# Tile 0 normalised in two halves, and three of its products in front of tile 1's turns

## The chip, the cores and the metric

The kernel runs on one core of a Trainium2 chip. The metric is the device time of one execution in microseconds (us); lower is better. The core has five engines that run on their own and wait for each other through semaphores: TensorE (PE, matmuls and transposes), VectorE (DVE), ScalarE (ACT), GpSimd (POOL) and SyncE (SP), which here issues most DMAs. Each engine works through its own queue in the order in which the program gives it work; an instruction that waits holds up everything behind it in that queue.

## The reference

The input x is 2048 tokens by 512 features. It is normalised over its features, and two blocks read the result: linear attention with 32 heads of 16, and a two-layer perceptron with a squared ReLU of width 1376. Both are added to x.

```python
xn = _layernorm(x)                                 # (x - mean) / sqrt(var + 1e-5)
q, k, v = split(xn @ wqkv)                         # 32 heads of 16
phi = lambda t: where(t > 0, t + 1, exp(t)) + 1e-6
kv  = einsum("bhsd,bhse->bhde", phi(k), v)
num = einsum("bhqd,bhde->bhqe", phi(q), kv)
den = einsum("bhqd,bhd->bhq", phi(q), phi(k).sum(s)) + 1e-6
A   = (num / den) @ wo
h   = xn @ w1 + b1
B   = square(max(h, 0)) @ w2 + b2
out = x + A + B
```

## The kernel before

All matmuls on the long path take their operands as a high and a low part (`fp32r` tiles, the low one the rest of the value), and a product is the sum of three passes: high by high, low by high, high by low. `split`, `heads_k`, `rests_k` and `transposed` make such parts: ACT or DVE copies the high one, DVE or POOL subtracts it for the low one.

The 2048 tokens are 16 tiles of 128 (`NT`), in blocks of four. The program has three stages: a start that brings in the first tiles, a loop over the tiles 2 to 15 (line 787) that projects k and sums k times tokens into four banks (`kx`), and two rounds of q, perceptron and output over two blocks each. The order on every engine is written out by hand: there is no planner, and an instruction stands in its engine's queue where the program calls it.

The change lies in the start. What happens there, with the lines:

- Eleven matmuls on zeros (L515), seen in the trace as 22, keep PE at work while the first loads are under way. The loads go through SP: tiles 0 and 1, the k columns of `wqkv` in four chunks (`rk`), tiles 2 and 3.
- `measure` (L230, L231) takes a tile's mean and variance on DVE. `roots` (L241, L242) makes one over the root of variance plus 1e-5 on POOL, as a power of -0.5.
- `normalise` (L264) subtracts the mean and multiplies by the root on DVE, one instruction for a tile of 128 by 512.
- `turned_pe` (L304) turns a tile with four transposes on PE. For tiles 0 and 1 they go into two banks of two chunks each, so that what follows can start on half a tile. It also sets the tile's last column to one (`ones`, L342, on POOL), behind the transposes.
- `transposed` gives three functions for a tile: `high(k)` copies half k of the turned tile on ACT (L320), `low(k)` subtracts that copy from it on DVE (L323), `keep_t` copies the whole for a store to memory (L330).
- `heads_k(j)` makes the high part of chunk j of the k weights (L562; chunk 0 on DVE, the others on ACT), `rests_k` its low part (L566; chunk 0 on POOL, the others on DVE).
- `some(i, u, js)` multiplies part u (0 high, 1 low) of tile i by the high part of the weight chunks in `js`, `rest(j, ...)` the high part of the tile by the low part of chunk j. Each is one matmul of 128 by 512 for a chunk, all into the bank `pk` of the tile.
- A copy of one element on POOL (L591) writes tile 1's result into the buffer of the tiles 4 to 7, so that the load of these tiles, which follows on SP, waits for it.
- Behind this stand the products of tile 2, `phi_k` (exponential and ReLU of k), `tokens` and `parts` (high and low parts of the normalised tile and of phi(k)), and `kx(0)`, the first sum (L385).

Of the kernel before, what the change touches and what calls it, by code (L numbers as in the profile page):

```python
# [10 lines left out]
OP = mybir.AluOpType  # L11
# [7 lines left out]
def kernel(  # L19
# [30 lines left out]
    nc = tc.nc  # L50
    xf = x.rearrange("b s d -> (b s) d")
    of = out.rearrange("b s d -> (b s) d")
    S, D = xf.shape
# [49 lines left out]
    def gjc(ap):  # L103

        return ap.rearrange("p (j g c) -> p g j c", j=NJ, g=NJ)
# [3 lines left out]
    def copy(eng, o, i, bias=0.0):  # L109
        if eng == "act":  # L110
            nc.scalar.activation(o, i, AF.Copy, bias=bias)  # L111
        elif bias:
            ENG[eng].tensor_scalar(o, i, bias, None, op0=OP.add)
        else:
            ENG[eng].tensor_copy(o, i)
# [41 lines left out]
    def load_x(i, t):  # L157
        n = t.shape[1]
        nc.sync.dma_start(t, xf[i * P:(i + n) * P, :].rearrange("(i p) d -> p i d", i=n))
        for k in range(n):  # L160
            xr[i + k] = t[:, k]
# [82 lines left out]
    def normalise(tiles, st, mv, y):  # L244

        n = len(tiles)
        r, u = (y[:, k, :n] for k in range(2))
        if tiles[-1] >= NPE:

            nc.vector.scalar_tensor_tensor(u, mv[:, :n, 0], -1.0, r, op0=OP.mult, op1=OP.mult)  # L250
        later = []

        def last(i, o, src, k):
            nc.scalar.activation(o, src, AF.Identity, bias=u[:, k:k + 1], scale=r[:, k:k + 1])
            if i in groups:
                regroup(i)

        for k, i in enumerate(tiles):
            o, src = xp[i], xr[i]
            if i >= NDVE:  # L260

                o, src = o.rearrange("p g (j c) -> p g j c", j=NJ), gjc(src)
            if i < NPE:
                nc.vector.tensor_scalar(o, src, mv[:, k, 0:1], r[:, k:k + 1], op0=OP.subtract, op1=OP.mult)  # L264
                if i in groups:
                    regroup(i)
            else:
                later.append(lambda a=(i, o, src, k): last(*a))
        return later
# [3 lines left out]
    def regroup(i):  # L273

        src, G = groups[i]
        via = dram.tile([P, NJ, src.shape[-1]], F32, name=f"via{i}")
        nc.sync.dma_start(via, src)
        of_g = via.rearrange("(r t) g n -> g t r n", r=NJ)
        for g in range(NJ):
            moves.append((G[32 * g:32 * (g + 1)], of_g[g]))  # L280
# [27 lines left out]
    def transposed(i, n=1):  # L308

        b, at = i // TB, slot(i)  # L310
        if i < NDVE:
            t = turned_pe(i, n)
        else:
            t = [xT[b][:, :, at] if i >= NPE else w512(f"t{i}", "p", 6).rearrange("p (j t) -> p j t", j=NJ)]
            turn(t[0], xg[i])
        m = NJ // n
        h, l = ([x[:, k * m:(k + 1) * m, at] for k in range(n)] for x in cols(i))

        def high(k=0):
            nc.scalar.activation(h[k], t[k], AF.Copy)  # L320

        def low(k=0):
            nc.vector.tensor_tensor(out=l[k], in0=t[k], in1=f32(h[k]), op=OP.subtract)  # L323

        def keep_t():
            o = t[0]
            if i < NDVE:
                o = w512(f"t{i}", "p", 6).rearrange("p (j t) -> p j t", j=NJ)
                for k in range(n):
                    copy("act", o[:, k * m:(k + 1) * m], t[k])  # L330
            if i < NPE:
                nc.sync.dma_start(xTd[b][:, :, at], o)

        return high, low, keep_t
# [27 lines left out]
    def project(i, ps, w, steps, first=True, last=True):  # L362

        for n, (j, u, v) in enumerate(steps):
            nc.tensor.matmul(ps, lhsT=cols(i)[u][:, j, slot(i)], rhs=w[v][:, j, :], start=first and n == 0,  # L365
                             stop=last and n == len(steps) - 1)
# [172 lines left out]
    for i0 in range(0, NT, TB):  # L539
# [6 lines left out]
        if i0 < NPE:  # L546
            i = i0 + TB - n - 1
# [3 lines left out]
        o = work.tile([P, n, 512], F32, name=f"xg{i0}", tag="r0" if i0 + TB == NT else "r3" if i0 >= NPE else "rc")  # L551
        for k in range(0, n, 2):
            i = i0 + TB - n + k
# [6 lines left out]
    def heads_k(*js, eng="act"):  # L560
        for j in js:
            copy(eng, wk[0][:, j, :], rk[:, j])  # L562

    def rests_k(eng, *js):
        for j in js:
            ENG[eng].tensor_tensor(out=wk[1][:, j, :], in0=rk[:, j], in1=f32(wk[0][:, j, :]), op=OP.subtract)  # L566
# [3 lines left out]
    def some(i, u, js, first=False):  # L570
        project(i, pks[i], wk, [(j, u, 0) for j in js], first, False)
# [6 lines left out]
    for t in two_tiles:  # L578
        measure(t)
        roots(*t)  # L580
    normalise(*two_tiles[0])
    high, low, keep0 = transposed(0, 2)
    high()
    heads_k(0, eng="dve")
    rests_k("pool", 0)
    some(0, 0, (0,), True)
    normalise(*two_tiles[1])
    high1, low1, keep1 = transposed(1, 2)
    heads_k(1)

    nc.gpsimd.tensor_copy(x4[:, 0, :1], xp[1][:, :1])  # L591
    load_x(4, x4)
    some(0, 0, (1,))
    low()
    some(0, 1, (0, 1))
    high(1)
    high1()
    low(1)
# [15 lines left out]
    some(1, 0, (2,))  # L614
    rest(1)
    normalise(*third)
    rests_k("dve", 2)
    some(1, 1, (2,))
# [8 lines left out]
    high, low, keep2 = transposed(2)  # L627
# [159 lines left out]
    for i in range(2, NT):  # L787
# [15 lines left out]
        if i < NDVE:  # L803
            high, low, keep_t = transposed(i + 1)
# [104 lines left out]
    for n in range(2):  # L909
# [124 lines left out]
        for p in range(NO + 1):  # L1034
            at_p = AT[p]
            kind, k = order[p] if p < NO else ("", 0)
            fa, fb = 2 * k, 2 * k + 1

            was, k = order[p - 1] if p else ("", 0)
# [209 lines left out]
        for e, f in enumerate(waiting[:-2]):  # L1249
# [14 lines left out]
            if n == 0 and 1 <= e < 5:  # L1264
                k, u = divmod(e - 1, 2)
# [68 lines left out]
```

## Time and profile before

| | before |
|---|---|
| median of 3 runs | 413.56 us (413.45 to 413.88) |
| profiled execution | 413.58 us |
| its span, first to last instruction | 411.9 us |
| granted TensorE clock | 1.00 |
| PE busy | 407.2 us (99%) |
| PE weight loads busy | 336.8 us (82%) |
| DVE busy | 311.1 us (76%) |
| ACT busy | 265.2 us (64%) |
| POOL busy | 59.0 us (14%) |
| data moved by DMA | 55.15 MB, mean 134 GB/s |

The profile is that of one execution. Its page gives the busy time of each engine, the chain of work that ended last, and groups of instructions. The views used here are the list of waits (which engine sat idle until which other was done), the table by stage (busy time of each engine between two times), the groups by line and shape, and the timeline: one row for each instruction or for several alike in a row, with start, duration, engine, line, operation, what is written and what is read, shape, count, and in brackets idle time of the engine before it with what ended it. Times in the timeline count from the start of the span. A line is often that of a helper, so the tile's name tells more than the line does.

### The profile page before, as it was taken

The page shows a single profiled execution, that of the slowest core. Times are in us where ns is not written, and L with a number is a line of the kernel's source. Part 1 is how long each engine was busy: PE and PEld are TensorE (multiplying, and loading weights), DVE is VectorE, ACT ScalarE, POOL GpSimd, SP SyncE. Part 2 cuts the span into 40 slices and gives each one's busy share as a digit, 9 for nine tenths or more (in the row PEclk, how much of TensorE's full clock was granted, in tenths as well). Part 3 has the DMA queues.
Part 4 walks back from the last instruction along what each step waited for, and adds up shares of the span by engine and source line. Part 5 has one row for each costly group of instructions (what it writes and reads, how often), then busy time and mean ns, then how long its engine had stood idle before and what let it go on. Part 6 is the DMA issues. An engine that isn't in the chain of part 4 may idle for free.

```text
span 411.9 us, 5395 instructions
## 1 busy us (share of the span) xinstructions
PE 407.2 (99%) x1831; PEld 336.8 (82%) x1831; DVE 311.1 (76%) x555; ACT 265.2 (64%) x465; POOL 59.0 (14%) x91
## 2 busy tenths in 40 slices
PE   8999999999999999999999999999999999999996
PEld 7788888888888888888878888888888888878885
DVE  5885567797899898988449995567989686449843
ACT  4757677656678779788637631577588857737520
POOL 5542233230410000030000140100000200000210
PEclk9999999999999999999999999999999999999999
DMA  6979672810412221273366992411121880024602
GB/s 221 344 230 338 171 306 103 254 28 2 124 60 71 79 73 56 77 198 58 134 237 241 382 183 87 118 53 51 51 78 28 231 197 32 2 98 157 103 1 102
DMA packets 45661, 55.15 MB, mean 134 GB/s; under 512 B 8001, under 2 KB 29761, under 8 KB 44354
## 3 DMA queue, kind: packets, MB, share of 16 engines
q1 hardware_dynamic: 43330, 50.61, 37.3%
q0 software_dynamic: 2304, 4.20, 6.4%
q8 instruction: 14, 0.23, 0.2%
q14 instruction: 13, 0.11, 0.1%
HBM read 41.43 MB, written 13.37 MB: 133 GB/s over the span
## 4 chain that ended last, share of the span: by engine, by line
PE 98%; DMA 1%; DVE 0%; POOL 0%; issue 0%; ACT 0%
PE acc L130 37%; PE b L484 32%; PE pk L365 11%; PE kx L385 11%; PE acc L495 2%; PE pz L130 1%; PE pkv L885 1%; PE pm L130 1%; PE pz0b L130 1%; PE b L130 1%; DMA x<-in_A_x_dram 1%; PE pt L304 1%; PE acc L502 0%; PE end L130 0%; DVE st L230 0%; POOL y L242 0%
## 5 line engine op out<-in xcount | busy, mean ns | idle before, releaser
L130 PE MATMUL acc<-w2r,s 128*128 128x512 f32 x477 | 112.8, 390 | 0.0
L130 PEld LDWEIGHTS acc<-w2r,s 128*128 128x128 f32 x477 | 89.4, 188 | 19.3 <-issue 0.7
L484 PE MATMUL b<-T,aop 128*128 128x512 f32 x336 | 83.4, 389 | 0.0
L484 PEld LDWEIGHTS b<-T,aop 128*128 128x128 f32 x336 | 63.1, 188 | 13.2
L385 PE MATMUL kx<-pk,tok 128*128 128x512 f32 x192 | 46.5, 391 | 0.0
L385 PEld LDWEIGHTS kx<-pk,tok 128*128 128x128 f32 x192 | 35.8, 188 | 7.7 <-ACT pk L111 0.3
L1015 POOL DMA_DIRECT2D res<-in_B_b_dram x16 | 14.3, 1123 | 181.5 <-DVE dt L426 64.2
L484 PE MATMUL b<-xs0h,aop 128*128 128x512 f32 x112 | 36.9, 390 | 0.0
L130 PE MATMUL acc<-mh,aTsr 128*128 128x512 f32 x112 | 35.6, 389 | 0.0
L1023 DVE TENSOR_TENSOR res<-acc,res 128x512 f32<-128x512 f32 x16 | 11.0, 692 | 23.0 <-PE acc L130 18.4
L119 POOL TENSOR_TENSOR tok<-xp,tok 128x512 fp32r<-128x512 f32 x16 | 21.2, 1327 | 43.2 <-ACT tok L111 43.2
L122 DVE TENSOR_TENSOR w2r<-r,w2r 128x512 fp32r<-128x512 f32 (+2 forms) x35 | 25.6, 734 | 0.1
L484 PEld LDWEIGHTS b<-xs0h,aop 128*128 128x128 f32 x112 | 21.0, 188 | 4.4
L130 PEld LDWEIGHTS acc<-mh,aTsr 128*128 128x128 f32 x112 | 21.0, 188 | 4.4
L111 ACT ACTIVATE aop<-S 128x512 fp32r<-128x512 f32 x28 | 17.5, 623 | 11.0 <-DVE S L714 11.0
L119 DVE TENSOR_TENSOR aop<-S,aop 128x512 fp32r<-128x512 f32 x28 | 19.5, 697 | 4.8 <-ACT aop L111 4.4
L119 DVE TENSOR_TENSOR s<-c,s 128x512 fp32r<-128x512 f32 x20 | 13.6, 689 | 11.5 <-ACT s L111 11.5
L130 PE MATMUL acc<-ml,aTsr 128*128 128x512 f32 x56 | 21.8, 389 | 0.0
L484 PE MATMUL b<-xs0l,aop 128*128 128x512 f32 x56 | 21.8, 389 | 0.0
L111 ACT ACTIVATE w2r<-r 128x512 fp32r<-128x512 f32 x32 | 19.6, 619 | 2.4 <-DMA out_dram<-res 2.0
L111 ACT ACTIVATE T<-Tf 128x512 fp32r<-128x512 f32 x16 | 9.5, 624 | 16.5 <-DVE Tf L657 16.4
L484 PE MATMUL b<-xs1h,aop 128*128 128x512 f32 x56 | 19.5, 389 | 0.0
(195 smaller groups left out, 769.3 us busy)
## 6 DMA issues: line engine op xcount, KB each, us to landing
r<-in_B_w_dram SPq DMA_DIRECT2D x49, 256.0 KB, 2.9
res<-in_A_x_dram SPq DMA_DIRECT2D x8, 512.0 KB, 4.6
res<-in_B_b_dram POOLq DMA_DIRECT2D x16, 256.0 KB, 5.5
out_dram<-res SPq DMA_DIRECT2D x15, 256.0 KB, 2.1
via<-xp SPq DMA_DIRECT2D x5, 512.0 KB, 3.0
xg<-via SPq DMA_DIRECT2D x20, 128.0 KB, 2.6
xTd<-t SPq DMA_DIRECT2D x8, 256.0 KB, 4.3
x<-in_A_x_dram SPq DMA_DIRECT2D x4, 512.0 KB, 6.9
```

Of the source, the lines that this page charges most:

```text
L111: nc.scalar.activation(o, i, AF.Copy, bias=bias)
L119: ENG[el].tensor_tensor(out=l, in0=src, in1=f32(h), op=OP.subtract)
L122: nc.vector.tensor_tensor(out=l, in0=src, in1=f32(h), op=OP.subtract)
L130: nc.tensor.matmul(ps, lhsT=a[u], rhs=b[v], start=first and n == 0, stop=last and n == 2)
L304: nc.tensor.transpose(t[k][:, at:at + P], xp[i][:, j * P:(j + 1) * P], ident)
L365: nc.tensor.matmul(ps, lhsT=cols(i)[u][:, j, slot(i)], rhs=w[v][:, j, :], start=first and n == 0, stop=last and n == len(steps) - 1)
L385: nc.tensor.matmul(kxp[c], lhsT=tok[i][:, u, c * P:(c + 1) * P], rhs=pk[i][:, v], start=i == 0 and (u, v) == first, stop=i == NT - 1 and ( ...
L484: nc.tensor.matmul(ps, lhsT=a[u][:, j * P:(j + 1) * P], rhs=b[v][:, j, :], start=first and j == 0 and n == 0, stop=last and j == 1 and n == 2,
L495: nc.tensor.matmul(ps, lhsT=s[u][:, k * P:(k + 1) * P], rhs=w2s[NF - 1][u][:, a:z], start=first and u == 0, stop=stop and u == 1)
L885: nc.tensor.matmul(ps[:, at], lhsT=wvs[:, c, at], rhs=kxs[c // 2][:, c % 2, at], start=c == 0 and j == 0, stop=c == NJ - 1 and j == NJ - 1 ...
L1015: nc.gpsimd.dma_start(r[:, i], b2[None, :].partition_broadcast(P), accum_op=OP.add)
L1023: nc.vector.tensor_tensor(out=r[:, a:z], in0=ps, in1=r[:, a:z], op=OP.add)
```

## The change

Two things are changed, both in the start. In `normalise`, tile 0 is done as two instructions of 256 columns each, where every other tile stays one instruction. In the written order, three products of tile 0 (low by weight chunk 0, high by weight chunk 1, after the high by chunk 0 that already stood there) come in front of tile 1's norm and turns, and with them `low()`, the subtraction for the first half of tile 0, which stands on DVE in front of tile 1's norm; `heads_k(1)` is called ahead of these products. The fourth product (low by chunk 1) stays behind tile 1's turns.

```diff
@@ normalise @@
             if i < NPE:
-                nc.vector.tensor_scalar(o, src, mv[:, k, 0:1], r[:, k:k + 1], op0=OP.subtract, op1=OP.mult)
+                for part in (slice(0, D // 2), slice(D // 2, D)) if i == 0 else (slice(None),):
+                    nc.vector.tensor_scalar(o[:, part], src[:, part], mv[:, k, 0:1], r[:, k:k + 1],
+                                            op0=OP.subtract, op1=OP.mult)
                 if i in groups:
                     regroup(i)
@@ the start @@
     heads_k(0, eng="dve")
     rests_k("pool", 0)
     some(0, 0, (0,), True)
+    low()
+    some(0, 1, (0,))
+    heads_k(1)
+    some(0, 0, (1,))
     normalise(*two_tiles[1])
     high1, low1, keep1 = transposed(1, 2)
-    heads_k(1)
 
     nc.gpsimd.tensor_copy(x4[:, 0, :1], xp[1][:, :1])
     load_x(4, x4)
-    some(0, 0, (1,))
-    low()
-    some(0, 1, (0, 1))
+    some(0, 1, (1,))
     high(1)
     high1()
     low(1)
```

## The prediction

> **What bounds the kernel now.** I read the page first, then the waits of the first 30 us, then a table by stage, then the timelines of the first 17 us, one engine at a time.
>
> ```profile
> span 411.9 us, 5395 instructions
> ...
> PE 98%; DMA 1%; DVE 0%; POOL 0%; issue 0%; ACT 0%
> ```
>
> The span is 411.9 us and the profiled run took 413.58 us, so 1.68 us lie outside the span; the median of the three runs, 413.56, is 0.02 us below the profiled run. TensorE (PE) carries 98% of the chain that ended last. The change touches only the first 9 us, so the question is whether PE waits anywhere near it, and whether it could make up a delay later.
>
> ```profile
> PEld pk L365 <- ACT xs1h L320: 0.7, 2, 0.5
> ...
> PEld kx L385 <- ACT pk L111: 0.3, 1, 0.3
> ...
> PE pk L365 <- ACT xs1h L320: 0.3, 1, 0.3
> PE pt L304 <- DVE xp L264: 0.2, 1, 0.2
> ```
>
> Apart from the start of the warm-up these are the only waits of PE and its weight loads (PEld) in that stretch, and all stand before the first kx matmul: the transposes of tile 0 wait for its norm, the first k product and later the first of tile 2 for ACT's copy, and kx(0) for ACT's part of pk.
>
> ```profile
> 16.19:22.23 6.04, 6.04 (x29) 5.00 (x29) 5.08 (x10) 4.91 (x10) 2.92 (x5) 1.00 0.90 307
> 350.00:400.00 50.00, 50.00 (x226) 40.90 (x225) 32.88 (x56) 27.76 (x47) 5.12 (x6) 1.00 0.28 74
> ```
>
> From 16.19 us on, PE is busy for all of a stage (6.04 of 6.04, 50.00 of 50.00), at a granted clock of 1.00. So there is nothing in which a later start could be absorbed: **what the first kx matmul gains or loses, the kernel gains or loses**. Now the timelines (start, duration, then engine, line, operation).
>
> ```profile
> 0.83 4.85 PE L515 MATMUL warm<-const-float32-0.0 128*128 128x128 f32 x22 [0.83 <-PEq L1320]
> 5.88 0.66 PE L304 MATMUL pt<-ident,xp 128*128 128x128 f32 x4 [0.20 <-DVE xp L264]
> 6.79 0.50 PE L365 MATMUL pk<-wkh,xs1h 128*128 128x512 f32 x1 [0.26 <-ACT xs1h L320]
> 7.13 0.60 PE L304 MATMUL pt<-ident,xp 128*128 128x128 f32 x4
> 7.49 0.47 PE L365 MATMUL pk<-wkh,xs1h 128*128 128x512 f32 x1
> ...
> 8.49 0.40 PE L365 MATMUL pk<-wkh,xs1h 128*128 128x512 f32 x1
> ...
> 16.19 3.02 PE L385 MATMUL kx<-pk,tok 128*128 128x512 f32 x12
> ```
>
> ```profile
> 5.28 0.55 DVE L264 TENSOR_SCALAR xp<-x,mv,y 128x512 f32<-128x512 f32 x1 [0.23 <-POOL y L242]
> 5.74 0.42 DVE L115 CAST wkh<-rk 128x512 fp32r<-128x512 f32 x1
> 6.30 0.55 DVE L264 TENSOR_SCALAR xp<-x,mv,y 128x512 f32<-128x512 f32 x1
> 6.77 0.42 DVE L323 TENSOR_TENSOR xs1l<-pt,xs1h 128x256 fp32r<-128x256 f32 x1
> 7.56 0.83 DVE L323 TENSOR_TENSOR xs1l<-pt,xs1h 128x256 fp32r<-128x256 f32 x2 [0.37 <-ACT xs1h L320]
> 8.50 0.69 DVE L230 BATCH_NORM_STATS2 st<-x 128x6 f32<-128x512 f32 x1
> ...
> 10.75 0.55 DVE L264 TENSOR_SCALAR xp<-x,mv,y 128x512 f32<-128x512 f32 x1 [0.43 <-POOL y L242]
> 11.21 1.28 DVE L566 TENSOR_TENSOR wkl<-rk,wkh 128x512 fp32r<-128x512 f32 x2
> 12.42 0.69 DVE L230 BATCH_NORM_STATS2 st<-x 128x6 f32<-128x512 f32 x1
> ...
> 14.32 0.55 DVE L264 TENSOR_SCALAR xp<-x,mv,y 128x512 f32<-128x512 f32 x1 [0.42 <-POOL xp L342]
> 14.79 0.68 DVE L360 SCALAR_TENSOR_TENSOR k<-pk,k 128x512 f32<-128x512 f32 x1
> 15.39 0.68 DVE L230 BATCH_NORM_STATS2 st<-x 128x6 f32<-128x512 f32 x1
> ```
>
> ```profile
> 6.36 0.38 ACT L320 ACTIVATE xs1h<-pt 128x256 fp32r<-128x256 f32 x1 [4.29 <-PE pt L304]
> ...
> 15.50 0.63 ACT L111 ACTIVATE pk<-k 128x512 fp32r<-128x512 f32 x1 [0.45 <-DVE k L360]
> ```
>
> ```profile
> 5.53 0.73 POOL L242 TENSOR_TENSOR y<-y,power 128x1 f32<-128x1 f32 x1
> 6.60 0.28 POOL L342 MEMSET xp<- 128x1 f32 x1 [0.34 <-PE pt L304]
> 6.69 1.30 POOL L566 TENSOR_TENSOR wkl<-rk,wkh 128x512 fp32r<-128x512 f32 x1
> ...
> 10.15 0.57 POOL L242 TENSOR_TENSOR y<-y,power 128x1 f32<-128x1 f32 x1
> ...
> 13.72 0.57 POOL L242 TENSOR_TENSOR y<-y,power 128x1 f32<-128x1 f32 x1
> ```
>
> Read backwards from kx(0) at 16.19: it waits for ACT's high half of pk at 15.50, that for VectorE's (DVE's) phi at 14.79, which stands behind the norm of tile 3 at 14.32, which waits for POOL's power at 13.72 to 14.29; POOL waits for the statistics of tile 3 at 12.42; these stand behind the two rests of wk from 11.21 and the norm of tile 2 at 10.75, which waits for POOL's power at 10.15 to 10.72; and that for the statistics of tile 2 at 8.50. From 8.50 to 16.19 DVE and POOL pass work to each other without slack. PE's own work ends just ahead and then waits 0.3 us. So **the start of tile 2's statistics (8.50 us) decides**. In DVE's queue it stands behind the low halves of tile 0 and tile 1 (6.77 and 7.56), and the last of these needs tile 1's norm (6.30), its transposes (7.13) and ACT's copy.
>
> **The change, part by part.**
>
> *Two halves of tile 0's norm.* One instruction more on DVE. No row shows a 256-wide norm; the form's ends are 512 elements (0.55 at 5.28) and the nearest small one:
>
> ```profile
> L1106 DVE TENSOR_SCALAR zc<-zc 128x4 f32<-128x4 f32 x2 | 0.3, 156 | 0.0
> ```
>
> A line between 0.156 for 4 and 0.55 for 512 gives 0.35 for 256. It cannot be under 0.28, half of the whole; the 256-wide subtraction at 6.77, with a PSUM source, took 0.42, which is the other end. I take 0.35, since it is the same operation. Neighbours overlap by 0.09 (5.74 against 5.83), so the halves end at 5.63 and 5.89. The warm matmuls end at 5.68 (0.83 + 4.85); transposes came 0.05 behind the norm, so the first two start at 5.68 instead of 5.88, the last two at 5.94, and all four end near 6.32 instead of 6.54. ACT's copy moves from 6.36 to 6.16 and ends at 6.54; the first k product moves from 6.79 to 6.59. The cast of wk at 5.74 moves to 5.80 and ends at 6.22, still ahead of 6.59: nothing lost. So far a gain of 0.20 us on PE.
>
> *Tile 0's low half in front of tile 1's norm.* It needs ACT's copy, so it starts 0.03 behind it, at 6.57. Behind it in DVE's queue stand tile 1's norm, both other low halves, tile 2's statistics and so the whole chain above. The norm started at 6.30 and can now start only 0.41 behind the low half (the spacing of the pair at 7.56), at 6.98: 0.68 later, for a norm that depends on nothing in that low half.
>
> *What the norm meets there.* POOL's 1.30 us subtraction (L566, the rest of wk chunk 0) ran from 6.69 to 7.99, just after the norm. It stands behind the memset of tile 0's ones column, 0.06 behind the end of the transposes; with these at 6.32, the memset is at 6.38, the subtraction at 6.47 to 7.77. So the norm, which came in front of it, now comes in the middle of it. What that costs is shown by two other pairs of rows:
>
> ```profile
> 17.88 1.29 POOL L119 TENSOR_TENSOR tok<-xp,tok 128x512 fp32r<-128x512 f32 x1 [1.46 <-ACT tok L111]
> 18.74 0.98 DVE L373 SCALAR_TENSOR_TENSOR pk<-k,pk 128x512 fp32r<-128x512 f32 x1
> ```
>
> ```profile
> L373 DVE SCALAR_TENSOR_TENSOR pk<-k,pk 128x512 fp32r<-128x512 f32 x11 | 7.6, 690 | 3.1 <-ACT pk L111 2.7 <-PE kx L385 0.2
> ```
>
> The usual duration of that DVE form is 0.69; beside a POOL subtraction that ended at 19.17 it took 0.98 and ended at 19.72, 0.55 behind it. It had been held until POOL was through, with 0.14 of its 0.69 done before. The other way round:
>
> ```profile
> L342 POOL MEMSET xp<- 128x1 f32 x16 | 1.7, 109 | 0.3 <-PE pt L304 0.3
> ```
>
> A memset of one column takes 0.109 in the mean; the one at 6.60 took 0.28 and ended at 6.88, 0.04 behind tile 1's norm. So a norm on DVE and work on POOL exclude each other. No row shows a norm as the one held; a plain bound below is that it isn't held (0), above that it waits to POOL's end and then needs 0.41 (0.55 less 0.14). I take held, because the norm itself held POOL at 6.60. What is left after POOL's end lies between 0.28 (half of 0.55) and 0.41; I take 0.35. The norm ends at 7.77 + 0.35 = 8.12 instead of 6.85, 1.27 late.
>
> The Trainium skill's page "SBUF — State Buffer", section "Who interferes with whom", speaks against this change at just this place: VectorE and GpSimd share one pair of ports, a tensor_scalar between SBUF tiles can run in a mode that takes it, and whichever issued first keeps it for its whole instruction. By that rule the sum is the one made here; the rows above agree with it for the subtraction held by POOL and for the memset held by the norm.
>
> *Three products in front of tile 1's turns.* The same number of matmuls; PE meets the second product at 6.59 + 0.34 = 6.93 (the first spacing, 6.79 to 7.13) and waits for the low half until 6.57 + 0.42 + 0.05 = 7.04, with two products and the turns queued behind it. The third product needs ACT's wk chunk 1, which follows the first copy on ACT as before. Both are through by about 7.6, and PE then waits for tile 1's norm until 8.17. That waiting is no cost by itself; it matters through what follows.
>
> *The sum.* ACT's copy of tile 0 came 0.48 behind the first transpose (5.88 to 6.36) and takes 0.38: tile 1's at 8.65 to 9.03. Its low half starts at 9.06, and tile 2's statistics 0.40 behind that, at 9.46 instead of 8.50: **0.96 late**. Every link from there to kx(0) keeps its length, so kx(0) starts at 17.15. PE's own delay is less (the first product of tile 1 at 9.08 instead of 8.49, 0.59 late) and hides in that wait. With 0.96 on the profiled run: 413.58 + 0.96 = 414.54, and 414.5 as a median. With the ends of the two unknown durations (halves 0.28 and 0.42, the rest of the held norm 0.28 and 0.41) it is 0.85 to 1.2, that is 414.4 to 414.8.
>
> *What moves along at no price.* POOL's ones column of tile 1 and the one-element copy that releases the load of tiles 4 to 7 wait for tile 1's turns, so SyncE issues that load about 1 us later, with the stores of the turned tiles and the later x loads behind it in SP's queue.
>
> ```profile
> x<-in_A_x_dram SPq DMA_DIRECT2D x1, 1024.0 KB, 5.2
> ```
>
> Its issue was at 8.18, and 5.2 makes it land at 13.4; its first reader is at 15.39. With both 1 us later the cover of 2 us stays; without it, each us late would go to kx(0). ACT's wk chunks 2 and 3 come behind tile 1's copies and about 1 us late, with PE late as well.
>
> There is one more thing that could collide: POOL's power for tile 1 (5.53) took 0.73 beside the norm and the cast. If it slips in between the two halves, the second half waits up to 0.3 us, everything behind it too: 414.8 to 414.9.
>
> **The rivals.**
>
> First, **the norm isn't held** by POOL. For it: no row shows a norm held. Against it: the memset at 6.60. Then the norm runs from 6.98 to 7.53, the turns at 7.58, ACT's copy at 8.06 to 8.44, the low half at 8.47, the statistics at 8.87: 0.37 late, 413.9. This is slower still, but by less than can be told.
>
> Second, the other side, **no slower: PE decides the start**. The place is the stretch between tile 2's statistics and kx(0). The three products let PE work while tile 1 is late, and its first product is 0.20 us earlier; if the chain DVE-POOL had 0.96 us to spare there, kx(0) would come 0.20 earlier, 413.4. It decides from the point at which that spare exceeds the delay of the statistics. For it: PE's only wait in the stretch before kx(0) is 0.3 us and some of 0.2. Against it: the norms at 10.75 and 14.32 each follow POOL's power by 0.03 us, which is no spare at all.
>
> Third, **the clock falls back**. The 22 warm matmuls (128 columns) took 4.85 us, 0.22 each, the four transposes from 7.13 to 7.49, 0.09 each, so the clock opened in between, after about 4.5 us of work. PE now has a gap of some 0.6 us before tile 1's turns. If it closed there and needed 4.5 us again, half of that is lost: 2.3 us more, 416.8. Against it: gaps of 0.2 and 0.3 us at this place left the granted clock at 1.00. The Trainium skill's page "TensorE: Matmul & The Clock Gate", section "HAM oscillation — how this bites in real kernels", names gaps beyond about 3.4 us as what closes it; by that rule nothing closes here.
>
> That the change isn't what it says cannot be: the built order of each engine has the two halves, the three products and the norm behind the low half, as written.
>
> **How the numbers follow.** The forecast (held) has a chance of 0.81, of which about 0.1 is for the collision of the power; the norm not held 0.14; PE decides 0.03; the clock 0.02. The difference that a measurement of this kernel can tell from none is about 0.2%, 0.83 us, so slower begins at 414.39. Of the forecast's 0.81 I give 0.07 to a sum just under that. Slower: 0.74 + 0.02 = 0.76. Within: 0.14 + 0.03 + 0.07 = 0.24, less 0.02 kept for a gain of over 0.83 us, which no case here gives, so 0.22. The range goes down to the case not held, 413.9, and up to the collision with a margin of 0.1, 415.0.
>
> **What would show it.** In the profile after: the two halves about 0.35 each; the first transposes at 5.7; tile 1's norm starting near 7.0 with a duration of over 1 us instead of 0.55, ending 0.3 to 0.4 behind POOL's L566; tile 2's statistics near 9.5; kx(0) near 17.2; PE without a gap from there. If the norm takes 0.55 beside POOL, the forecast is wrong and 413.9 right. If the statistics are late and kx(0) is not, PE or another engine sets the start. If PE shows gaps or slower matmuls after 18 us, the argument that nothing later changes is wrong.

## The result, and the profile after

| | before | after |
|---|---|---|
| median of 19 runs each | 413.93 us (413.44 to 415.78) | 414.96 us (414.60 to 417.00) |
| profiled execution | 413.58 us | 414.79 us |
| its span | 411.9 us | 413.1 us |

The ratio after to before is 1.0029, 95% interval 1.0016 to 1.0042: the kernel became slower, by 1.03 us between the medians and by 0.7 to 1.7 us by that interval. The page of after, with the chain that ended last, and the waits of PE's weight loads:

```profile
span 413.1 us, 5396 instructions
...
PE 95%; DVE 2%; POOL 1%; DMA 1%; issue 0%; ACT 0%
```

```profile
PEld pt L306 <- DVE xp L265: 1.2, 2, 0.9
...
PEld kx L387 <- ACT pk L111: 0.6, 1, 0.6
```

PE fell from 98% to 95% of the chain; DVE, which had rounded to 0%, has 2%. The wait for tile norms is now 1.2 us in two pieces, and the wait in front of kx(0) is 0.6 us instead of 0.3. The timelines of the start (start, duration, engine, line, operation; the file is three lines longer, so L264 is L265, L323 is L325, L566 is L568 and so on):

```profile
5.93 0.76 PE L306 MATMUL pt<-ident,xp 128*128 128x128 f32 x4 [0.17 <-DVE xp L265]
6.84 0.50 PE L367 MATMUL pk<-wkh,xs1h 128*128 128x512 f32 x1
7.30 0.50 PE L367 MATMUL pk<-wkh,xs1l 128*128 128x512 f32 x1
7.64 0.39 PE L367 MATMUL pk<-wkh,xs1h 128*128 128x512 f32 x1
8.47 0.66 PE L306 MATMUL pt<-ident,xp 128*128 128x128 f32 x4 [0.44 <-DVE xp L265]
...
17.39 3.06 PE L387 MATMUL kx<-pk,tok 128*128 128x512 f32 x12
```

```profile
5.46 0.74 DVE L265 TENSOR_SCALAR xp<-x,mv,y 128x256 f32<-128x256 f32 x2 [0.23 <-POOL y L242]
...
6.82 0.42 DVE L325 TENSOR_TENSOR xs1l<-pt,xs1h 128x256 fp32r<-128x256 f32 x1 [0.29 <-ACT xs1h L322]
7.17 1.25 DVE L265 TENSOR_SCALAR xp<-x,mv,y 128x512 f32<-128x512 f32 x1
...
9.37 0.42 DVE L325 TENSOR_TENSOR xs1l<-pt,xs1h 128x256 fp32r<-128x256 f32 x1 [0.62 <-ACT xs1h L322]
9.71 0.68 DVE L230 BATCH_NORM_STATS2 st<-x 128x6 f32<-128x512 f32 x1
```

```profile
6.76 0.10 POOL L344 MEMSET xp<- 128x1 f32 x1 [0.19 <-PE pt L306]
6.85 1.28 POOL L568 TENSOR_TENSOR wkl<-rk,wkh 128x512 fp32r<-128x512 f32 x1
```

Tile 1's norm starts at 7.17, behind the low half at 6.82, and takes 1.25 us instead of 0.55. POOL's subtraction (L568) runs from 6.85 to 8.13; the norm ends at 8.42, 0.29 us behind it. Then everything follows in a row: tile 1's turns at 8.47 (7.13 before), the statistics of tile 2 at 9.71 (8.50), kx(0) at 17.39 (16.19). In this execution the first load landed 0.18 us later, so tile 0's norm starts at 5.46 instead of 5.28. I therefore measure from that norm to kx(0), and call it the distance: 10.91 us before, 11.93 after, **1.02 more**. It stays to the end:

```profile
17.39:60.00 42.61, 42.61 (x191) 35.24 (x192) 29.10 (x56) 28.45 (x50) 17.00 (x28) 1.00 0.78 271
```

In this row PE is busy for all of the stretch, as before, and from kx(0) to the end of the last matmul it is 392.29 us, against 392.26 before.

### The profile page after: what moved, and what is told of

Read it like the earlier page. It is cut to its first block, busy times and chain, and to the rows that moved or that the text cites. A ratio compares the mean times of both kernels' runs of the same rounds, so it can differ in the third digit from the quotient of the medians.

```text
span 413.1 us, 5396 instructions
## 1 busy us (share of the span) xinstructions
PE 407.9 (99%) x1831; PEld 336.5 (81%) x1831; DVE 311.4 (75%) x556; ACT 265.0 (64%) x465; POOL 58.8 (14%) x91
## 4 chain that ended last, share of the span: by engine, by line
PE 95%; DVE 2%; POOL 1%; DMA 1%; issue 0%; ACT 0%
PE acc L130 37%; PE b L486 32%; PE kx L387 11%; PE pk L367 9%; PE acc L497 2%; PE pz L130 1%; PE pkv L888 1%; PE pm L130 1%; PE pz0b L130 1%; PE b L130 1%; DMA x<-in_A_x_dram 1%; DVE xp L265 1%; DVE st L230 0%; PE pt L306 0%; POOL y L242 0%
```

## The experiments

Each is told with its distance, which is read from one profile, and with the ratio of its times to before. The time alone tells half a microsecond badly: its 95% intervals are 0.2% to 0.4% wide. The rows of a profile are good to a few hundredths, but one execution can differ from another by 0.1 to 0.25 us of distance, by when a load lands (told with the first experiment) and by the pace of the first transposes (told at the end).

### The halves alone

```diff
-                nc.vector.tensor_scalar(o, src, mv[:, k, 0:1], r[:, k:k + 1], op0=OP.subtract, op1=OP.mult)
+                for part in (slice(0, D // 2), slice(D // 2, D)) if i == 0 else (slice(None),):
+                    nc.vector.tensor_scalar(o[:, part], src[:, part], mv[:, k, 0:1], r[:, k:k + 1], ...)
```

> Before, with tile 0's norm in two halves and nothing else. The measure is the distance from the start of tile 0's norm to the start of kx(0): 10.91 us before, 11.93 after. Theory (tile 1's norm is late behind the low half and then held by POOL): no cost here; the first turns come 0.13 earlier, tile 2's statistics still start near 8.5, distance 10.9 within 0.1, time within 0.3 us of before. Rival (a second instruction and the later cast cost most of it): distance 11.3 or more.

DVE and POOL in this run:

```profile
6.53 0.55 DVE L265 TENSOR_SCALAR xp<-x,mv,y 128x512 f32<-128x512 f32 x1
...
8.50 0.69 DVE L230 BATCH_NORM_STATS2 st<-x 128x6 f32<-128x512 f32 x1
```

```profile
6.68 0.10 POOL L344 MEMSET xp<- 128x1 f32 x1 [0.18 <-PE pt L306]
6.77 1.45 POOL L568 TENSOR_TENSOR wkl<-rk,wkh 128x512 fp32r<-128x512 f32 x1
```

Distance 10.82 (kx(0) at 16.20), ratio 1.0003 (0.9991 to 1.0014). The halves show no cost, and no gain that the times could tell: the first turns come 0.13 us earlier against the norm, but tile 2's statistics start at 8.50 as before.

What the statistics wait for there is not the low half in front of them. Before, the two low halves end at 8.39 (7.56 + 0.83) and the statistics start 0.11 us behind them; in after they start at 9.71, 0.08 ahead of the end of that subtraction at 9.79. What comes last is the load of tile 2, which the semaphore events of the traces put at 8.48 in both executions. So the low halves had about 0.19 us in hand in the kernel before, and a delay of them shows only beyond that. The distance is 0.09 shorter here because tile 0's norm started 0.10 later and the load landed at the same time.

Here tile 1's norm (6.53 to 7.08) is in front, takes its 0.55, and it is POOL's subtraction that is stretched, 1.45 instead of 1.30 us. The second instruction is not where the time went. One row doesn't fit a norm that shuts POOL out from its first moment: the memset at 6.68, 0.15 us into the norm, takes its usual 0.10, where the one before, 0.30 us into the norm (6.60 against 6.30), was held to its end. So it seems to be the later part of the norm that excludes POOL.

### The order alone

```diff
-                for part in (slice(0, D // 2), slice(D // 2, D)) if i == 0 else (slice(None),):
-                    ...
+                nc.vector.tensor_scalar(o, src, mv[:, k, 0:1], r[:, k:k + 1], op0=OP.subtract, op1=OP.mult)
```

(against after: one piece again)

> After, with tile 0's norm in one piece again: the order alone. Theory: tile 1's norm starts near 7.2, is held to 0.29 us behind POOL's L566 (ends about 8.3, over 1.0 long), tile 2's statistics near 9.6, distance norm to kx(0) about 12.0, time 1.0 to 1.2 us over before. Rival (the halving costs most of it): distance 11.3 or less.

```profile
7.55 1.21 DVE L264 TENSOR_SCALAR xp<-x,mv,y 128x512 f32<-128x512 f32 x1
...
10.05 0.68 DVE L230 BATCH_NORM_STATS2 st<-x 128x6 f32<-128x512 f32 x1
```

```profile
6.07 0.98 PE L304 MATMUL pt<-ident,xp 128*128 128x128 f32 x4 [0.20 <-DVE xp L264]
...
17.73 3.06 PE L385 MATMUL kx<-pk,tok 128*128 128x512 f32 x12
```

Distance 12.27, ratio 1.0034 (1.0023 to 1.0046), and the norm takes 1.21 us: the order alone costs all that the change costs. The 0.27 over the expected 12.0 lies mostly in tile 0's turns, where four transposes took 0.98 us instead of 0.66; more on that at the end.

### Only the low half in front of the norm

```diff
     some(0, 0, (0,), True)
+    low()
     normalise(*two_tiles[1])
...
     some(0, 0, (1,))
-    low()
     some(0, 1, (0, 1))
```

(against before: one call moved; the products keep their places)

> Before, with only the low half of tile 0 called in front of tile 1's norm; the norm in one piece, the products in the order of before. Theory: as much as the whole change, tile 1's norm over 1.0 long, distance about 12.0, since the products that moved stand under a wait anyway. Rival (the products in front of tile 1's turns on PE cost it): distance 11.3 or less.

```profile
5.92 1.12 PE L304 MATMUL pt<-ident,xp 128*128 128x128 f32 x4
7.08 0.50 PE L365 MATMUL pk<-wkh,xs1h 128*128 128x512 f32 x1
8.80 0.66 PE L304 MATMUL pt<-ident,xp 128*128 128x128 f32 x4 [1.22 <-DVE xp L264]
...
16.90 1.09 PE L365 MATMUL pk<-wkh,xs1l 128*128 128x512 f32 x4
17.83 2.96 PE L385 MATMUL kx<-pk,tok 128*128 128x512 f32 x12
```

```profile
7.40 1.35 DVE L264 TENSOR_SCALAR xp<-x,mv,y 128x512 f32<-128x512 f32 x1
...
10.04 0.68 DVE L230 BATCH_NORM_STATS2 st<-x 128x6 f32<-128x512 f32 x1
```

Distance 12.51, ratio 1.0029 (1.0013 to 1.0044). One call on DVE gives the whole loss without any product being moved; the rival, that the loss needs the products in front of the turns, is out. What the products cost by themselves is in the next experiment. The distance came 0.5 over the expected one. The turns took 1.12 us here (0.25 more until ACT could start), and PE ran through to kx(0) without a wait, with kx(0) 7.79 us behind tile 2's statistics where the other runs have 7.7: with the products behind the turns PE itself has become the later one. So the moved products seem to help by about 0.1, once the norm is late anyway; that is one profile.

### The norm back in front

```diff
     some(0, 0, (0,), True)
+    normalise(*two_tiles[1])
     low()
     some(0, 1, (0,))
     heads_k(1)
     some(0, 0, (1,))
-    normalise(*two_tiles[1])
     high1, low1, keep1 = transposed(1, 2)
```

(against after)

> After, with tile 1's norm in front of the low half again; halves and products stay as in after. Theory: the norm is 0.55 long and starts near 6.4 (as counted before), but the turns now stand on PE behind two products of which one waits for the low half, so they start near 7.85 instead of 7.13 and tile 2's statistics near 9.15; distance about 11.5. Rival (the place of the norm on DVE is all): distance 10.9.

```profile
6.96 0.50 PE L367 MATMUL pk<-wkh,xs1h 128*128 128x512 f32 x1
7.66 0.50 PE L367 MATMUL pk<-wkh,xs1l 128*128 128x512 f32 x1 [0.20 <-DVE xs1l L325]
...
8.23 0.60 PE L306 MATMUL pt<-ident,xp 128*128 128x128 f32 x4
...
17.08 3.02 PE L387 MATMUL kx<-pk,tok 128*128 128x512 f32 x12
```

```profile
6.73 0.55 DVE L265 TENSOR_SCALAR xp<-x,mv,y 128x512 f32<-128x512 f32 x1
...
9.40 0.68 DVE L230 BATCH_NORM_STATS2 st<-x 128x6 f32<-128x512 f32 x1
```

Distance 11.50 as expected, ratio 1.0023 (1.0013 to 1.0034). The norm is 0.55 again and early (6.73), but tile 1's turns wait on PE behind the product at 7.66, which waits for the low half, and start at 8.23. So there are two ways to be late here: behind the low half on DVE, and behind its product on PE, which costs 0.59 us of distance (11.50 against 10.91) although the norm is early. In after the first hides the second.

### The norm late, but POOL idle

```diff
     heads_k(0, eng="dve")
-    rests_k("pool", 0)
...
     nc.gpsimd.tensor_copy(x4[:, 0, :1], xp[1][:, :1])
+    rests_k("pool", 0)
     load_x(4, x4)
...
-    rest(0, 0)
     some(1, 0, (0,), True)
-    rest(0, 1)
     some(1, 0, (1,))
...
     some(1, 0, (2,))
+    rest(0)
     rest(1)
```

(against after)

> After, with POOL's subtraction for weight chunk 0 (L566 of before) moved behind tile 1's turns, and its two products moved behind the other products of weight chunk 2's high part; nothing is left out. So tile 1's norm still stands behind the low half, but POOL is idle when it runs. Theory: the norm takes 0.55 and ends about 0.6 earlier than in after, tile 2's statistics 0.4 behind before, distance norm to kx(0) about 11.3 (10.91 before, 11.93 after). Rival (the norm is slow for another reason): over 1.0 long as in after, distance 11.9.

```profile
7.21 0.54 DVE L265 TENSOR_SCALAR xp<-x,mv,y 128x512 f32<-128x512 f32 x1
...
9.15 0.68 DVE L230 BATCH_NORM_STATS2 st<-x 128x6 f32<-128x512 f32 x1
```

```profile
8.82 1.29 POOL L568 TENSOR_TENSOR wkl<-rk,wkh 128x512 fp32r<-128x512 f32 x1
```

```profile
7.69 0.45 PE L367 MATMUL pk<-wkh,xs1h 128*128 128x512 f32 x1
7.98 0.60 PE L306 MATMUL pt<-ident,xp 128*128 128x128 f32 x4
```

The norm starts at 7.21, at the place that it has in after, and takes 0.54 us: it is long only when POOL's subtraction is under way. Distance 11.35, expected 11.3. So of the 1.02 us, **0.58 went with the hold by POOL, and the other 0.44 is the rest of the new order**. The split is that of one execution, and the hold may be worth more: the norm itself ends 0.72 us earlier than in after (2.24 instead of 2.96 behind the start of tile 0's norm), but the turns start 0.23 behind its end instead of 0.05, since on PE they stand behind the third product at 7.69. The ratio, 1.0023 (1.0010 to 1.0036), doesn't tell this kernel from after, and its median, 415.20, is even higher; its profile has a wait of about 1.1 us that after's hasn't, told at the end. Its lowest run, 413.99, is 0.61 under the lowest of after, 414.60, which fits but is another set of runs. So the 0.58 rests on the profile.

### POOL's subtraction twice

```diff
-    rests_k("pool", 0)
+    rests_k("pool", 0, 0)
```

(against after)

> After, with POOL's subtraction for weight chunk 0 done twice in a row into the same place. Theory, held for one instruction: the norm gets in between the two, is about 1.25 long as in after, distance 11.9, and the second subtraction is the one that waits. Rival (POOL keeps what it holds while it has work queued): the norm about 2.5 long, distance about 13.2.

```profile
7.21 1.25 DVE L265 TENSOR_SCALAR xp<-x,mv,y 128x512 f32<-128x512 f32 x1
...
9.75 0.69 DVE L230 BATCH_NORM_STATS2 st<-x 128x6 f32<-128x512 f32 x1
```

```profile
6.89 2.70 POOL L568 TENSOR_TENSOR wkl<-rk,wkh 128x512 fp32r<-128x512 f32 x2
```

The norm takes 1.25 us as in after, with 2.70 us of POOL work queued from 6.89 on. It got in when the first subtraction was done: POOL holds it for one instruction, not for its queue. Distance 12.07, expected 11.9, and one run only, without an interval. The statistics start 4.24 us behind tile 0's norm, as in after (4.25); the 0.14 more comes behind them, where PE waits for POOL's second subtraction.

### Two tries for a faster start

```diff
-    load_k(*range(NJ))
-    t = two("x2")
-    for i in range(2):
-        load_x(2 + i, t[:, i:i + 1])
+    load_k(0, 1)
+    t = two("x2")
+    load_x(2, t[:, :1])
+    load_k(2, 3)
+    load_x(3, t[:, 1:])
...
     low()
+    third = statistics(2)
+    roots(*third)
     some(0, 1, (0, 1))
...
-    third = statistics(2)
-    roots(*third)
     heads_k(2)
```

(against the halves alone)

> Before, with the norm of tile 0 in halves, tile 2 loaded after the second weight chunk, and its statistics and root in front of tile 0's second low half, in DVE's gap. Theory (the chain of DVE and POOL from tile 2's statistics sets kx(0)): the statistics start over 1 us earlier, the wait in front of kx(0) goes, PE sets the stretch, distance 10.5 to 10.6, time 0.3 to 0.4 us under before. Rival (the chain has slack, PE sets it already): distance 10.9.

```profile
7.35 0.69 DVE L230 BATCH_NORM_STATS2 st<-x 128x6 f32<-128x512 f32 x1
...
14.00 0.54 DVE L265 TENSOR_SCALAR xp<-x,mv,y 128x512 f32<-128x512 f32 x1
14.76 0.69 DVE L362 SCALAR_TENSOR_TENSOR k<-pk,k 128x512 f32<-128x512 f32 x1 [0.22 <-ACT k L360]
```

```profile
7.01 0.50 PE L367 MATMUL pk<-wkh,xs1h 128*128 128x512 f32 x1 [0.26 <-ACT xs1h L322]
...
16.25 1.58 PE L387 MATMUL kx<-pk,tok 128*128 128x512 f32 x6
```

Tile 2's statistics start at 7.35 instead of 8.50, and tile 3's norm at 14.00 is 0.32 earlier, but phi at 14.76 waits for ACT's exponential instead. Distance 10.84, kx(0) at 16.25, ratio 0.9990 (0.9972 to 1.0009): no change that can be told. **My theory of 0.3 to 0.4 us failed here**, though not cleanly. From the first k product to kx(0) it is 9.24 us (7.01 to 16.25), and 9.44 with the halves alone (6.76 to 16.20); so about 0.2 is gained there. But in this execution ACT's copy came 0.69 us behind the start of the first transposes instead of 0.48, and that takes the 0.2 back. The wait in front of kx(0), 0.3 us before, is still 0.2 us. Then the second try:

```diff
     some(1, 1, (2,))
-    for i in range(2):
-        for u in range(2):
-            some(i, u, (3,))
     keep0()
     keep1()
+    high, low, keep2 = transposed(2)
+    high()
     rests_k("dve", 3)
     fourth = statistics(3)
     roots(*fourth)
-    high, low, keep2 = transposed(2)
-    high()
     low()
+    for i in range(2):
+        for u in range(2):
+            some(i, u, (3,))
```

(against the first try)

> The kernel with early statistics of tile 2 (tile 0 in halves, tile 2 loaded and measured earlier), and with tile 2's turns, its high and low parts and tile 3's statistics called in front of the four products of weight chunk 3. Theory (with the chain out of the way, what stood ahead of kx(0) was ACT: copy of tile 2's turns, then ReLU and exponential of tile 0's k): ACT's copy comes 0.9 us earlier, PE's waits of 0.2 us in front of tile 2's first product and of kx(0) go, distance from the norm of tile 0 to kx(0) 10.4 to 10.5 (10.84 in the kernel with early statistics, of which about 0.2 is the clock that opened late), time about 0.4 us under before. Rival (PE's own products fill the stretch): distance 10.6 or more.

```profile
15.32 1.07 PE L367 MATMUL pk<-wkh,xs1l 128*128 128x512 f32 x4
16.23 2.98 PE L387 MATMUL kx<-pk,tok 128*128 128x512 f32 x12
```

```profile
11.85 0.60 ACT L322 ACTIVATE xs1h<-pt 128x512 fp32r<-128x512 f32 x1 [1.30 <-PE pt L306]
13.47 0.60 ACT L358 ACTIVATE k<-pk 128x512 f32<-128x512 f32 x1 [1.03 <-PE pk L367]
```

ACT's copy did come 0.9 us earlier (11.85), but its ReLU now waits for PE (13.47). Distance 10.77, ratio 0.9998 (0.9986 to 1.0011): the rival was right as far as one profile tells, PE's own products fill the stretch (9.39 us from the first k product to kx(0)). No version here beats the kernel before by what can be measured.

## Why the prediction was right or wrong

The mechanism was right where the change acts, with one link misread in the kernel before. By its own steps, counted from the start of tile 0's norm:

- **The halves.** I took 0.35 for one; they took 0.41, near the upper end:

```profile
L265 DVE TENSOR_SCALAR xp<-x,mv,y 128x256 f32<-128x256 f32 x2 | 0.7, 412 | 0.2 <-POOL y L242 0.2
```

  So the first turns gained 0.13 instead of 0.20 us, and their end 0.03, and POOL's subtraction started 1.39 behind the norm instead of 1.19.
- **The place of the norm.** Forecast at 1.70, found at 1.71. Two misses cancel in it, which is luck: the low half starts at 1.36 instead of 1.29, and the norm 0.35 behind it instead of 0.41.
- **The hold.** The rest after POOL's end was 0.29, I had taken 0.35 between 0.28 and 0.41. It is near the low end, half of 0.55: of a held norm less is left than I had taken from the held subtraction. Both misses together put the norm's end at 2.96 instead of 2.84.
- **What tile 2's statistics wait for.** I had them behind the low halves. In the profile before it is tile 2's load that comes last there, 0.19 us later than the low halves would allow (see the halves alone). The sum took 0.40 from the start of the last low half to the statistics; in after, where the load is long there, it is 0.34 (9.37 to 9.71). This took back half of the 0.12 above.
- **The rest of the chain.** Tile 2's statistics 4.25 instead of 4.18, kx(0) 11.93 instead of 11.87: 1.02 later than before, forecast 0.96. From the statistics to kx(0) it is 7.69 before and 7.68 after, 7.68 with the norm back in front, 7.72 with POOL idle: the part without slack, as I had read it.
- **The rivals.** The norm that isn't held is ruled out by the pair of after and the kernel with POOL idle. The clock did not fall back: the granted clock behind kx(0) is 1.00. "PE decides" is wrong for this change, since the distance grew; but the two tries show how near it was, with only 0.1 to 0.2 us to gain when the chain is out of the way.

The step that failed is the term that the sum starts from, the time of the kernel before: I took 413.58 for it, the profiled run, beside a median of 413.56 over three runs. Over 19 runs the median is 413.93. The forecast of 414.5 is 0.46 under the measured 414.96; 0.37 of this is that base, 0.09 the sum (0.94 forecast against medians, 1.03 measured). Set against the base of 19 runs, 414.5 says a change of only 0.57 us, little more than half of the 1.03 measured. Three runs that agreed within 0.43 us said nothing of the longer tail: 8 of the 19 lie above 414.2. The statement that nothing later in the kernel waits was read from a single execution that had no such wait; see below.

That 414.96 still lies under the 415.0 at the top of the range is luck. The room above 414.8 was meant for a collision in which POOL's power holds up the second half of tile 0's norm. It didn't come: the two halves took 0.74 together, with the second following the first without a gap.

The Trainium skill's page "SBUF — State Buffer", section "Who interferes with whom", has the first of the two to issue keep the shared ports for its instruction, while the other waits. The runs agree in both directions: the norm took 1.25 instead of 0.55 us behind POOL's start, POOL's subtraction 1.45 instead of 1.30 behind the norm's, and with two subtractions queued the norm waited for one. They differ on the whole instruction: the memset at 6.68 with the halves alone ran its 0.10 us inside the norm that had started at 6.53, so a memset that comes 0.15 us into a norm isn't kept out.

## What to carry to other kernels

An instruction that is moved in a queue takes the place of others there: ask for each one that it passes whether that one was free to start, and who waits for it; here a subtraction with 0.4 us of work pushed back a norm on which two more engines waited. Look too at what runs on the engine that shares a resource in the new place: the norm lost as much to the POOL instruction that it now meets (0.70 us, 1.25 instead of 0.55) as to the place that it now has (0.69 us later). Look, too, for a load that is the last to arrive before you count on an instruction in front. And take the base time from enough runs for a forecast as fine as this one.

## What the runs showed that I had not expected

**A wait that comes in some executions only.** With the halves alone, the profiled run took 414.73 us, 0.82 above that kernel's own median, although its kx(0) was not late. The loss stands at 50 us. DVE before, the same in the run with the halves alone, and that run's PE:

```profile
47.32 0.71 DVE L289 STREAM_TRANSPOSE xT<-xg 128x512 f32<-128x512 f32 x1 [1.98 <-DMA xg<-via]
```

```profile
49.34 0.71 DVE L291 STREAM_TRANSPOSE xT<-xg 128x512 f32<-128x512 f32 x1 [3.98 <-DMA xg<-via]
```

```profile
50.77 0.50 PE L367 MATMUL pk<-wkh,xs1h 128*128 128x512 f32 x1 [0.66 <-ACT xs1h L322]
```

The turn of a tile waits for its trip through memory (`xg<-via`). Before, this load released DVE after 1.98 us of idle time, and PE ran on without a gap; in the other run after 3.98, and PE's first product of that tile, at 49.93 before, came at 50.77. From kx(0) to the last matmul it is 392.26 us before, 393.41 there, and 393.34 with POOL idle, whose profile has the same wait. That is where about 1.1 us comes from in these two executions; that the slower single runs of each kernel have the same wait is likely but not shown, and why the load is late was not tried.

**The pace of the first transposes.** Four transposes took 0.66 us before, 0.98 and 1.12 in the second and third experiments, and ACT's copy came 0.72 behind their start in both instead of 0.48. That is 0.25 to 0.28 each, near the 0.22 of the warm-up matmuls. The table by stage says a granted clock of 1.00 for all of them, but it counts time for which the trace has no clock record as full. The records themselves begin, at the full clock, 5.36 us into the span before, and at 6.77 and 7.02 in the second and third experiments: before the first transposes at 5.88, and in the midst or at the end of those at 6.07 and 5.92. The Trainium skill's page "TensorE: Matmul & The Clock Gate", section "What's actually happening", says that the window of the clock gate runs free of the kernel, so that the opening moves from run to run, by 0.5 us either way. The traces agree that it moves, but further: over the ten profiles here the records begin between 3.93 and 7.02 us. Why it moves no run here shows. The late opening is worth 0.25 us of distance, a quarter of the effect under study.
